# Two token tiles of the output product as seven half-size block products

## The chip, the cores and the metric

One Trainium2 chip, of which this kernel uses one core. A core has TensorE (PE: matmuls, with its weight loads shown apart as PEld), VectorE (DVE), ScalarE (ACT), GpSimd (POOL) and SyncE (SP, which issues most of the transfers). The metric is the device time of one execution in microseconds (us); lower is better. Three runs of the kernel before gave 304.9, 305.29 and 306.08 us, median 305.29.

## The reference

Attention in which a query sees only the keys whose nearest centroid is the same as its own, then a two-layer network with the SiLU gate. There are 4 batches, 8 heads, 768 tokens, a head size of 64 and 16 centroids a head; the network goes from 512 to 2048 to 512.

```python
q_assign = np.argmax(np.einsum('bhsd,hcd->bhsc', q_n, c_n), axis=-1)
k_assign = np.argmax(np.einsum('bhsd,hcd->bhsc', k_n, c_n), axis=-1)
mask = q_assign[:, :, :, None] == k_assign[:, :, None, :]
scores = np.where(mask, scale * np.matmul(q, k.transpose(0, 1, 3, 2)), -1000000000.0)
attn = softmax(scores)
x = np.matmul(attn, v).transpose(0, 2, 1, 3).reshape(B * S, H * D)
h = x @ w_in
g = h * (1.0 / (1.0 + np.exp(-h)))
return (g @ w_out).astype(np.float32)
```

Here q_n, k_n and c_n are the rows divided by their lengths, and softmax stands for the reference's lines with the maximum taken off. All inputs and the output are float32; the kernel works in f16 with f32 sums.

## The kernel before

**Stages.** The work goes by half batches (b, c): batch b of 4, half c of 2, 384 query tokens each, so eight half batches. For each of them:

- *Preparation of a head* (a Job): `load` brings raw rows of q and k as f32 (tile raw, eight buffers). `hi` and `lo` split them into two f16 parts (tile hl), `xpose` turns them by a transposing DMA, `logits_1` multiplies with the centroids, `lsum`, `mx_n` and `ge_n` find the cluster. Its one-hot code goes into the transposed rows (tile ab), by `c_scale`, `c_xpose` and `c_move` for batches 2 and 3, by `cd_mm` and `cd_ev` otherwise. So the mask is part of the score matmul.
- *Scores* (`qk_mm`, line 343): 192 units, 24 a half batch, each of two matmuls of 384 columns, and `exp` (line 348) on ScalarE for each. Two PSUM buffers of two banks are used in turn.
- *Values* (`pv`, line 360): 36 matmuls of 65 columns for two heads. The 65th column is a column of ones of the value tile vt and gives the sum of the softmax. `norm` divides (lines 370 and 372), and `xn_d` (a transposing DMA) or `xn_t` and `xn_ev` (TensorE and a copy) turn the result into xt.
- *Gate blocks* (`unit_a`, line 410): 16 blocks of 128 of the 2048 inner features, four matmuls of 384 columns each. `tanh` (line 430, ScalarE) and `gate` (line 433, VectorE) give (tanh(h/2) + 1) * h, which is twice the SiLU value, into gt (two buffers, 16 x 384 elements a partition).
- *Output* (`part_b`, line 468): for each of three tiles t of 128 tokens, 16 matmuls of 512 columns (gt block as weights, wout_s as the moving side) add up in one PSUM bank, in four pieces of four matmuls. Line 475 multiplies by 0.5 into ot, and SyncE sends it (line 477).

**Order.** Nothing is ordered by the engines themselves: each executes its instructions in the order in which the program issues them, and the program is written out flat. The opening is a list by hand (`plan`, line 657) up to unit 27 and the first eight gate blocks. Then a planner in the same file takes over (lines 690 to 947). It keeps a clock for each engine, and `choice` takes the engine that can start next. For TensorE, `options` lists the pieces that could go: scores when due (by PACE, LEAST, GAIN and the stock of other work), values, gate blocks and output pieces, each with a rank, the time at which its inputs are there and a length. `add` puts a piece on another engine's lane with the time when it is ready and how late it may be. `date` ties loads, preparation and casts to a unit's number. `sent` counts an output's time on SyncE. Four PSUM banks are shared by ph, pO, po, px and psN (`bank`, `done`); `po_on` says whether an output tile is open. What remains at the end is issued by lines 948 to 993: the gate blocks of the last half batch in pairs (`unit_aa`), its outputs, and the very last tile in three column pieces.

Half batches use gt in turn: gate blocks of one cannot begin while outputs of the one two before are left (line 882).

Of the kernel before, what the change touches and what calls it, by code (L numbers as in the profile page):

```python
# [34 lines left out]
def kernel(  # L35
# [64 lines left out]
    raws, hls, abs_ = {}, {}, {}  # L100

    def load(job, eng=nc.sync):
        raw = mp.tile([128, 12, D], f32, name="raw", tag="raw", bufs=8)
        for dst, ap in job.srcs:
            o = raw[:, dst, :]
            if len(ap.shape) == 2:
                eng.dma_start(o.rearrange("p n d -> p (n d)"), ap)  # L107
            else:
                eng.dma_start(o.rearrange("p (h n) d -> p h (n d)", h=4), ap)
        raws[job.name] = raw  # L110

    def hi(job, eng=None, part=None):
        s = part or slice(0, job.n)
        if job.name not in hls:
            hls[job.name] = mp.tile([128, 12, 2, D], f16, name="hl", bufs=4)
        o, i = hls[job.name][:, s, 0, :], raws[job.name][:, s, :]
        if eng == "act":
            nc.scalar.activation(out=o, in_=i, func=AF.Copy, bias=0.0, scale=QS)  # L118
        elif eng == "pool":
            nc.gpsimd.tensor_scalar(out=o, in0=i, scalar1=QS, scalar2=None, op0=ALU.mult)  # L120
        else:
            nc.vector.tensor_scalar(out=o, in0=i, scalar1=QS, scalar2=None, op0=ALU.mult)  # L122
# [103 lines left out]
    def c_xpose(job):  # L226
        cd = cds[job.name] = mp.tile([128, 2, 128], f16, name="cdt", bufs=4)
        nc.sync.dma_start_transpose(cd, ohd[nn[job.name] % 3].rearrange("p h n -> p (h n)"))  # L228
# [16 lines left out]
    def cd_ev(job, eng):  # L245
        m = (job.n + 1) // 2
        cd = mp.tile([6 * HC, 256], f16, name="cd", bufs=4)
# [173 lines left out]
    def unit_a_end(b, c, fb, ph):  # L421
# [7 lines left out]
        def tanh():  # L429
            nc.scalar.activation(out=tn, in_=ph[:, 0:HALF], func=AF.Tanh, bias=0.0, scale=0.5)  # L430
# [12 lines left out]
    def unit_aa(b, c, fb):  # L443
# [8 lines left out]
        def act():  # L452
            tn = mp.tile([128, 2, HALF], f32, name="tn2", tag="raw", bufs=8)
            nc.scalar.activation(out=tn, in_=ph[:, :, 0:HALF], func=AF.Tanh, bias=0.0, scale=0.5)
# [8 lines left out]
    def part_b(b, c, t, n, bk=3):  # L463
# [9 lines left out]
        def act():  # L473
            ot = mp.tile([128, DM], f32, name="ot", bufs=3)
            nc.vector.tensor_scalar(out=ot, in0=po, scalar1=0.5, scalar2=None, op0=ALU.mult)  # L475
# [3 lines left out]
        return act  # L479

# [30 lines left out]
    for vt in vtb:  # L511
        nc.vector.memset(vt[:, :, D : D + 1], 1.0)
# [182 lines left out]
    PACE, LEAST, GAIN = 1.40, 12, .03  # L695
    HOLD = 6

# [23 lines left out]

    dates = {}
# [6 lines left out]
    def chain(job, b):  # L729
        def split(t):  # L730
# [4 lines left out]
            add("DVE", t, 0.5, lambda: hi(job), lambda t: add("DVE", t, 0.9, lambda: lo(job), turned, 1.5), 1.5)  # L735
# [19 lines left out]
        def out_of_bank(t):  # L755
            add("DVE", t + 0.2, 0.44, lambda: cd_ev(job, "D"), lambda t: known(max(clock["SP"], t) + 1.0), 0.3)
# [31 lines left out]
    for i in range(H, B * H):  # L788
# [8 lines left out]
        date(p, lambda t, i=i: cast(i, t))  # L797
    for od in ohd:
        date(60, lambda t, od=od: add("POOL", t, 0.3, lambda: nc.gpsimd.memset(od, 0.0)))
# [8 lines left out]
    turn, po_on = 0, None  # L808
# [6 lines left out]
    def norm_piece(n, t):  # L815
# [10 lines left out]
        def after(t):  # L826
            if by_dma(n):
                add("SP", t, 1.28, lambda: xn_d(i, c), lambda t: ready(lands(t, 0.61) + 1.5))
            else:
                tensor_todo.append((t + 0.06, 0.17, lambda: xn_t(i, c), lambda t: add("DVE", t + 0.2, 0.3, lambda: xn_ev(i, c, "D"), ready)))  # L830

        add("DVE", t + 0.2, 0.72, lambda: norm(i, c), after)

    def unit_piece():
# [3 lines left out]
        def gated(t):  # L838
            gate_at[b, c, fb] = t

        def then(t):
# [10 lines left out]
    def part_piece():  # L852
        nonlocal po_on
        it = qb.pop(0)
        f = part_b(*it, None)
        po_on = it[:3] if it[3] < 3 else None

        def then(t):
            if f:
                add("DVE", t + 0.2, 0.62, f, sent)  # L860

        return then

    def options(t):
# [20 lines left out]
        if qb and (po_on or bank_at is not None):  # L885
            b, c, t_, n = qb[0]
            need = [gate_at.get((b, c, fb)) for fb in range(4 * n, 4 * n + 4)]
            a_soon = qa and x_at[qa[0][:2]] <= t + 0.5
            if None not in need and (len(qb) > HOLD or not a_soon):
                found.append((3 if turn < 4 else 2, max(need + ([] if po_on else [bank_at])), 0.863, "b"))  # L890
        return found

    def tensor_piece(o):
# [17 lines left out]
        elif what in ("a", "b"):  # L911
            turn = (turn + 1) % 7
            box = []
            run("PE", r, length, lambda: box.append(unit_piece() if what == "a" else part_piece()), lambda t: box[0](t))
# [33 lines left out]
    late = []  # L948
    while qa:
# [3 lines left out]
        if qb:  # L953
            f = part_b(*qb.pop(0), None)
# [3 lines left out]
    for fb in range(0, NFB, 4):  # L958
        for n, unit in ((0, unit_aa), (2, unit_a), (3, unit_a)):
# [3 lines left out]
            if qb and n != 2:  # L963
                f = part_b(*qb.pop(0), None)
# [4 lines left out]
    for x in qb:  # L969
        f = part_b(*x, None)  # L970
# [10 lines left out]
    for w in (5 * DM // 8, DM // 4, DM // 8):  # L981
# [10 lines left out]
        nc.vector.tensor_scalar(out=ot[:, cs_], in0=po[:, 0:w], scalar1=0.5, scalar2=None, op0=ALU.mult)  # L992
# [29 lines left out]
```

## Time and profile before

| | |
|---|---|
| median of 3 runs | 305.29 us |
| profiled execution, span from first to last instruction | 302.8 us |
| matmuls of line 468 (output tiles), 368 of 512 columns | 90.8 us busy |
| matmuls of line 343 (scores), 384 of 384 columns | 93.2 us busy |
| matmuls of line 410 (gate blocks), 480 of 384 columns | 92.4 us busy |
| matmuls of line 360 (values), 1152 of 65 columns | 41.2 us busy |
| tanh (line 430) and gate (line 433), 120 each | 60.1 and 64.0 us busy |
| DMA | 44.07 MB, mean 146 GB/s |

The profile is of one execution and counts its time from the first instruction to the last; the runs' times hold also what lies around it. Matmuls overlap in the records: a row's mean is longer than the distance from one start to the next, so prices of matmuls are best taken from stretches where one kind stands alone. A row of the groups reads: line, engine, operation, output and input tiles, shapes, count, then busy time in us and the mean in ns, then the idle time of the engine before these instructions and what ended it. In the chain and the timeline, a row gives the start, the length and how many instructions were merged. A row of the waits gives who waited for whom, the total, how often, and the longest.

### The profile page before, as it was taken

The page shows a single profiled execution, that of the slowest core. Times are in us where ns is not written, and L with a number is a line of the kernel's source. Part 1 is how long each engine was busy: PE and PEld are TensorE (multiplying, and loading weights), DVE is VectorE, ACT ScalarE, POOL GpSimd, SP SyncE. Part 2 cuts the span into 40 slices and gives each one's busy share as a digit, 9 for nine tenths or more (in the row PEclk, how much of TensorE's full clock was granted, in tenths as well). Part 3 has the DMA queues.
Part 4 walks back from the last instruction along what each step waited for, and adds up shares of the span by engine and source line. Part 5 has one row for each costly group of instructions (what it writes and reads, how often), then busy time and mean ns, then how long its engine had stood idle before and what let it go on. Part 6 is the DMA issues. An engine that isn't in the chain of part 4 may idle for free.

```text
span 302.8 us, 7783 instructions
## 1 busy us (share of the span) xinstructions
PE 294.3 (97%) x3113; PEld 186.3 (62%) x3113; DVE 200.6 (66%) x427; ACT 211.2 (70%) x341; POOL 69.1 (23%) x131
## 2 busy tenths in 40 slices
PE   7899989999999999999999999999999999999995
PEld 3777756566675566655666556655666556755644
DVE  5987669699995679855889468873464136522732
ACT  5899889653985688955698468955897568951520
POOL 2984700101310141433333324122100000000000
PEclk9999999999999999999999999999999999999999
DMA  7888999999794879869999998953101120010102
GB/s 212 249 185 183 201 254 209 247 252 223 174 184 117 218 188 151 197 160 176 231 187 226 187 179 211 163 82 97 38 0 55 46 82 13 16 50 35 37 35 69
DMA packets 74387, 44.07 MB, mean 146 GB/s; under 512 B 54352, under 2 KB 69360, under 8 KB 74352
## 3 DMA queue, kind: packets, MB, share of 16 engines
q1 hardware_dynamic: 69264, 35.16, 50.8%
q0 software_dynamic: 4800, 8.13, 14.2%
q8 instruction: 24, 0.39, 0.6%
q10 hardware_dynamic: 288, 0.30, 0.3%
q14 instruction: 11, 0.09, 0.1%
HBM read 27.30 MB, written 6.29 MB: 111 GB/s over the span
## 4 chain that ended last, share of the span: by engine, by line
PE 87%; ACT 4%; DVE 4%; DMA 2%; SPq 1%; issue 1%; DVEq 0%; ACTq 0%
PE ph L410 25%; PE po L468 25%; PE pS L343 19%; PE pO L360 11%; PE psN L175 3%; ACT P L348 3%; PE phs L448 2%; DVE hl L127 1%; PE po L986 1%; DMA raw<-in_k_dram 1%; DMA xt<-xn 1%; SPq L107 1%; ACT ab L159 1%; PE px L382 0%; SPq L228 0%
## 5 line engine op out<-in xcount | busy, mean ns | idle before, releaser
L348 ACT ACTIVATE P<-pS 128x768 f16<-128x768 f32 x192 | 155.6, 821 | 55.1 <-PE pS L343 54.7
L343 PE MATMUL pS<-ab 128*128 128x384 f16 x384 | 93.2, 326 | 0.5 <-ACT P L348 0.4
L410 PE MATMUL ph<-xt,win_s 128*128 128x384 f16 x480 | 92.4, 326 | 1.2 <-DVE gt L433 0.8
L468 PE MATMUL po<-wout_s,gt 128*128 128x512 f16 x368 | 90.8, 379 | 0.0
L433 DVE SCALAR_TENSOR_TENSOR gt<-tn,ph 128x384 f16<-128x384 f32 x120 | 64.0, 549 | 23.7 <-ACT tn L430 23.1
L430 ACT ACTIVATE tn<-ph 128x384 f32<-128x384 f32 x120 | 60.1, 507 | 10.1 <-PE ph L410 8.1
L410 PEld LDWEIGHTS <-win_s 128*128 128x128 f16 x480 | 46.2, 98 | 31.4 <-issue 2.0
L468 PEld LDWEIGHTS <-gt 128*128 128x128 f16 x368 | 35.0, 98 | 33.8
L343 PEld LDWEIGHTS <-ab 128*128 128x128 f16 x384 | 34.7, 98 | 26.1 <-issue 1.1
L360 PEld LDWEIGHTS <-P 128*128 128x128 f16 x1152 | 39.8, 97 | 4.4
L360 PE MATMUL pO<-vt,P 128*128 128x65 f16 x1152 | 41.2, 193 | 0.0
L127 DVE SCALAR_TENSOR_TENSOR hl<-raw,hl 128x768 f16<-128x768 f32 (+3 forms) x35 | 31.9, 916 | 0.8 <-ACT hl L118 0.4
L475 DVE TENSOR_SCALAR ot<-po 128x512 f32<-128x512 f32 x23 | 15.8, 688 | 23.3 <-PE po L468 23.1
L290 POOL CAST vt<-vn 128x384 f16<-128x384 f32 x32 | 17.9, 558 | 46.4 <-DMA vn<-in_v_dram 41.9
L187 DVE TENSOR_REDUCE L<-psN 128x192 f32<-128x384 f32 (+1 forms) x27 | 14.9, 550 | 15.1 <-PE psN L175 15.0
L232 POOL DMA_DIRECT2D ab<-cdt x16 | 8.9, 557 | 58.0 <-PE pS L343 28.0
L175 PEld LDWEIGHTS <-ab 128*128 128x128 f16 x458 | 17.2, 97 | 5.0 <-DMA ab<-hl 1.1
L175 PE MATMUL psN<-stk,ab 128*128 128x32 f16 (+1 forms) x458 | 18.6, 188 | 0.5 <-DMA ab<-hl 0.5
L370 DVE RECIPROCAL zr<-pO 128x6 f32<-128x6 f32 x32 | 6.2, 193 | 19.2 <-PE pO L360 18.8
L372 DVE TENSOR_TENSOR xn<-pO,zr 128x384 f16<-128x384 f32 x32 | 17.8, 557 | 1.1
L219 POOL TENSOR_SCALAR od<-od 128x96 f16<-128x96 f16 x16 | 9.2, 576 | 36.0 <-DVE od L212 35.9
L122 DVE TENSOR_SCALAR hl<-raw 128x768 f16<-128x768 f32 x24 | 13.9, 580 | 0.6 <-DMA raw<-in_k_dram 0.6
(75 smaller groups left out, 155.8 us busy)
## 6 DMA issues: line engine op xcount, KB each, us to landing
raw<-in_k_dram SPq DMA_DIRECT2D x31, 192.0 KB, 3.8
out_dram<-ot SPq DMA_DIRECT2D x23, 256.0 KB, 2.3
raw<-in_q_dram SPq DMA_DIRECT2D x24, 192.0 KB, 3.6
vn<-in_v_dram SPq DMA_DIRECT2D x16, 192.0 KB, 4.5
vn<-in_v_dram POOLq DMA_DIRECT2D x16, 192.0 KB, 3.7
win_s<-in_moe_w_in_dram POOLq DMA_DIRECT2D x8, 256.0 KB, 6.7
wout_s<-in_moe_w_out_dram POOLq DMA_DIRECT2D x4, 512.0 KB, 18.2
raw<-in_q_dram SPq DMA_DIRECT2D x2, 384.0 KB, 4.3
```

The costliest lines, as they stand in the source:

```text
L127: nc.vector.scalar_tensor_tensor(out=hl[:, s, 1, :], in0=raws[job.name][:, s, :], scalar=QS, in1=hl[:, s, 0, :], op0=ALU.mult, op1=ALU.sub ...
L175: nc.tensor.matmul(L[:, n % g, :, n // g], ab[:, i, :], stk[:, job.groups[i // 3][0], x : x + w], start=(x == 0), stop=(x + w == 2 * HC),)
L290: nc.gpsimd.tensor_copy(vt[:, :, 0:D], vns.pop(i))
L343: nc.tensor.matmul(pS[:, e, 0:HALF], abs_[kj.name][:, kn, :], rhs, start=True, stop=True)
L348: nc.scalar.activation(out=P, in_=pst.pop(u)[:, :, 0:HALF], func=AF.Exp, bias=0.0, scale=ESC)
L360: nc.tensor.matmul(o[:, (2 * t + h) * VW : (2 * t + h + 1) * VW], Ps[i + h, c, j // 2][:, j % 2, ts(t, 128)], vtb[(i + h) % 13][:, j, 0:VW ...
L372: nc.vector.tensor_tensor(out=xn, in0=ov[:, :, 0:D], in1=zr.unsqueeze(2).to_broadcast([128, 2 * NM, D]), op=ALU.mult)
L410: nc.tensor.matmul(ph[:, 0:HALF], win_s[:, r, ts(fb, 128)], xts[b, c][:, r, :], start=(r == 0), stop=(r == NR - 1))
L430: nc.scalar.activation(out=tn, in_=ph[:, 0:HALF], func=AF.Tanh, bias=0.0, scale=0.5)
L433: nc.vector.scalar_tensor_tensor(out=gt[:, fb, :], in0=tn, scalar=1.0, in1=ph[:, 0:HALF], op0=ALU.add, op1=ALU.mult)
L468: nc.tensor.matmul(po, gts[b, c][:, fc, ts(t, 128)], wout_s[:, fc, :], start=(fc == 0), stop=(fc == NFB - 1))
L475: nc.vector.tensor_scalar(out=ot, in0=po, scalar1=0.5, scalar2=None, op0=ALU.mult)
```

## The change

For five of the eight half batches, (1,0) to (3,0), the first two of the three token tiles are computed together. Their 256 tokens x 2048 features times 2048 x 512 are cut into 2 x 2 blocks, and Strassen's scheme in Winograd's form gives the product by seven block products instead of eight, each of 8 matmuls of 256 columns. For this

- VectorE forms four sums of gt blocks a pair (`sums`): S1 and S2 in a new tile sg, S3 and S4 in place in gt;
- VectorE forms four differences of wout blocks once, in ten pieces from unit 72 on (`tw_piece`); they lie in five raw slots that later loads no longer use (these have three), and two of 32 blocks in zz;
- products add up in two PSUM banks, X and Y. ScalarE copies product 1 to ot (`p1`) and, after products 6 and 5, the whole of X to a tile uu (`u2`); VectorE adds them to the outputs (`c11`, `c22`, `c12`). Product 6 waits for `p1`, product 7 for `u2`, product 4 for `c22`, product 3 for `c22` and S4;
- the two tiles leave in two transfers, one of 512 columns side by side and one of two pieces of 256 columns a row. The third tile goes as before, and its pieces may be taken ahead of a product that is not ready.

The factor of a half moves: the column of ones in vt becomes 2.0, so that x is halved, tanh takes scale 1.0, and the outputs are copied without a factor. The planner may now put some casts and copies on ScalarE or VectorE (`either`), by which has less before it; four of its constants are changed. Tiles hl and cd share fewer buffers after the first 18 jobs. The list of the opening stays.

```diff
+    EARLY = H + 2 + H
+    def raw_tag(n):
+        return f"raw{n % 8 if n < EARLY else 5 + n % 3}"
...
-        raw = mp.tile([128, 12, D], f32, name="raw", tag="raw", bufs=8)
+        raw = mp.tile([128, 12, D], f32, name="raw", tag=raw_tag(n), bufs=1)
...
-            nc.scalar.activation(out=tn, in_=ph[:, 0:HALF], func=AF.Tanh, bias=0.0, scale=0.5)
+            nc.scalar.activation(out=tn, in_=ph[:, 0:HALF], func=AF.Tanh, bias=0.0, scale=1.0)
...
+    TW = ((0, 0, 6), (0, 6, 2), (1, 0, 4), (1, 4, 4), (2, 0, 2), (2, 2, 4), (2, 6, 2), (3, 0, 2), (3, 2, 4), (3, 6, 2))
...
+    def tw_piece(n, f, m):
+        if n * HK + f < 30 and len(tws) <= (n * HK + f) // 6:
+            tws.append(mp.tile([128, 6, HD], f16, name="tw", tag=f"raw{len(tws)}", bufs=1))
+        ks, us = slice(f, f + m), slice(HK + f, HK + f + m)
+        lo_, up = slice(0, HD), slice(HD, DM)
+        a = wout_s[:, ks if n == 0 else us, lo_ if n == 3 else up]
+        b_ = tw(0, f, m) if n == 2 else tw(2, f, m) if n == 3 else wout_s[:, ks, up if n else lo_]
+        nc.vector.tensor_tensor(out=tw(n, f, m), in0=a, in1=b_, op=ALU.subtract)
...
+        def sums(self, k):
...
+            o, x, y, op = (
+                (s1, a21, a22, ALU.add), (s2, s1, a11, ALU.subtract), (a21, a11, a21, ALU.subtract), (a12, a12, s2, ALU.subtract)
+            )[k - 1]
+            nc.vector.tensor_tensor(out=o, in0=x, in1=y, op=op)
+
+        def product(self, k):
+            gt, lo_, up = self.gt, slice(0, HD), slice(HD, DM)
+            if k == 1:
+                self.X = bank("po")
+            if k == 2:
+                self.Y = bank("po2")
+            o = self.Y[:, lo_] if k == 2 else self.X[:, up if k in (5, 3) else lo_]
+            for f in range(HK):
...
+                nc.tensor.matmul(o, w, x, start=(f == 0 and k in (1, 2)), stop=(f == HK - 1), skip_group_check=True)
+
+        def p1(self):
+            self.ot = mp.tile([128, DM], f32, name="ot", bufs=3)
+            nc.scalar.activation(out=self.ot[:, HD:DM], in_=self.X[:, 0:HD], func=AF.Copy, bias=0.0, scale=1.0)
+
+        def c11(self):
+            nc.vector.tensor_tensor(out=self.ot[:, HD:DM], in0=self.Y[:, 0:HD], in1=self.ot[:, HD:DM], op=ALU.add)
+            done(self.Y)
+
+        def u2(self):
+            nc.scalar.activation(out=uus[0][:, HD : HD + DM], in_=self.X, func=AF.Copy, bias=0.0, scale=1.0)
...
+        def c22(self):
+            nc.vector.tensor_tensor(out=self.ot[:, 0:HD], in0=self.X[:, 0:HD], in1=uus[0][:, DM : DM + HD], op=ALU.add)
+            o, x = self.rows()
+            nc.sync.dma_start(o[:, x + HD : x + HD + DM], self.ot)
+
+        def c12(self):
+            ot = mp.tile([128, DM], f32, name="ot", bufs=3)
+            nc.vector.tensor_tensor(out=ot, in0=self.X, in1=uus[0][:, 0:DM], op=ALU.add)
+            done(self.X)
...
-        nc.vector.memset(vt[:, :, D : D + 1], 1.0)
+        nc.vector.memset(vt[:, :, D : D + 1], 2.0)
...
-    PACE, LEAST, GAIN = 1.40, 12, .03
+    PACE, LEAST, GAIN, WORK = 1.34, 12, .03, 20.05
     HOLD = 6
+    MARGIN = 0.3
+    EARLY_T = 72
...
+    def backlog(eng, t):
+        return max(clock[eng] - t, 0.0) + sum(p[2] for p in lanes[eng] if p[0] <= t + 1.0)
+
+    def either(ready, dve, act, f, then=None, late=0.0):
+        eng = "ACT" if backlog("ACT", ready) + act + MARGIN < backlog("DVE", ready) + dve else "DVE"
+        add(eng, ready, act if eng == "ACT" else dve, lambda: f(eng[0]), then, late)
...
+    paired = {(b, c) for b in range(B) for c in range(2)} - {(0, 0), (0, 1), (B - 1, 1)}
...
-                qb.extend((b, c, t_, n) for t_ in range(NM) for n in range(4))
+                if (b, c) in paired:
+                    pairs[b, c], at[b, c] = Pair(b, c), {}
+                    qb.extend([(b, c, "p", k) for k in (1, 2, 6, 5, 7, 4, 3)] + [(b, c, NM - 1, n) for n in range(4)])
+                else:
+                    qb.extend((b, c, t_, n) for t_ in range(NM) for n in range(4))
...
+            names = {6: ("c1", "s2"), 5: ("s1",), 7: ("u2", "s3"), 4: ("c22",), 3: ("c22", "s4")}[n]
+            need = [at[b, c].get(x) for x in names] + [tw_ready(n)]
...
-        if unit < NU and unit - 2 in exp_at and 6 * pv_next > unit - 15:
+        if unit < NU and unit - 2 in exp_at and 6 * pv_next > unit - 11:
...
-                stock = 1.302 * len(qa) + 0.863 * len(qb) + 20.8 * (unit // 24 - released)
-                due = t >= scored + min(max(PACE + GAIN * (stock - LEAST - 0.867 * (24 - unit % 24)), 0.8), 2.2)
+                stock = 1.253 * len(qa) + 0.868 * len(qb) + WORK * (unit // 24 - released)
+                due = t >= scored + min(max(PACE + GAIN * (stock - LEAST - WORK / 24 * (24 - unit % 24)), 0.8), 2.2)
...
+            ahead = next((k for k, q in enumerate(qb) if (q[2] == "p") != (qb[0][2] == "p")), None)
+            for k in (0, ahead):
+                if k is not None and (k or opened or len(qb) > HOLD or not a_soon):
+                    r = part_ready(qb[k], bank_at)
+                    if r is not None:
+                        found.append((3.5 if k else 3 if turn < 4 else 2, r, 0.874 if qb[k][2] == "p" else 0.863, ("b", k)))
```

More of the change, by code (lines that the diff above doesn't have):

```diff
@@ L839, in gated @@
             gate_at[b, c, fb] = t
+            if fb == NFB - 1 and (b, c) in paired:
+                if all("over" in at[x] for x in pairs if x != (b, c)):
+                    sums_from(b, c, t)
+                else:
+                    next_pair.append((b, c))
         def then(t):
@@ L948, with tail_part @@
     late = []
+    def tail_part():
+        it = qb.pop(0)
+        if it[2] != "p":
+            return part_b(*it, None)
+        pr, k = pairs[it[:2]], it[3]
+        if k in (2, 6, 7, 4):
+            while late:
+                late.pop(0)()
+        pr.product(k)
+        return {1: pr.p1, 2: lambda: (pr.c11(), pr.sums(4)), 5: pr.u2, 7: pr.c22, 3: pr.c12}.get(k)
     while qa:
```

149 lines of the change are left out of this document (121 added, 28 removed).

## The prediction

> **What bounds the kernel now.** I read the page's busy table, then the chain that ended last, then the busy time by stages, and last TensorE's waits. From the page:
>
> ```profile
> span 302.8 us, 7783 instructions
> PE 294.3 (97%) x3113; PEld 186.3 (62%) x3113; DVE 200.6 (66%) x427; ACT 211.2 (70%) x341; POOL 69.1 (23%) x131
> PE 87%; ACT 4%; DVE 4%; DMA 2%; SPq 1%; issue 1%; DVEq 0%; ACTq 0%
> ```
>
> TensorE is named first by both. A busy share can hide idle stretches, so here is the busy time in stages of about one half batch each (length, then PE, PEld, DVE, ACT and POOL busy, clock, DMA share, GB/s):
>
> ```profile
> 36.00:65.00 29.00, 28.16 (x280) 17.57 (x277) 21.96 (x43) 21.94 (x37) 2.16 (x5) 1.00 1.19 234
> 65.00:98.00 33.00, 32.74 (x349) 20.86 (x348) 28.61 (x61) 22.73 (x37) 4.92 (x11) 1.00 0.83 186
> 98.00:131.00 33.00, 33.00 (x392) 21.73 (x390) 26.91 (x55) 26.37 (x42) 9.97 (x19) 1.00 0.86 184
> 131.00:164.00 33.00, 32.34 (x343) 20.19 (x342) 23.74 (x47) 24.34 (x39) 13.25 (x25) 1.00 0.96 200
> 164.00:197.00 33.00, 33.00 (x331) 20.34 (x327) 23.97 (x48) 23.39 (x38) 9.68 (x22) 1.00 0.91 186
> 197.00:230.00 33.00, 33.00 (x327) 20.48 (x326) 17.49 (x36) 24.44 (x42) 4.91 (x11) 1.00 0.24 53
> 230.00:264.00 34.00, 34.00 (x311) 20.52 (x309) 14.52 (x28) 25.39 (x42) 0.00 (x0) 1.00 0.14 44
> ```
>
> From 36 to 264 us TensorE is idle for 0.84 + 0.26 + 0.66 = 1.76 us, and the granted clock is 1.00. So in these stages nothing but TensorE sets the pace, and a matmul taken away there is worth its whole length, as long as the planner keeps the engine fed. Its waits after the opening, and the chain's last pieces:
>
> ```profile
> PE ph L410 <- DVE gt L433: 0.8, 1, 0.8
> PE psN L175 <- DMA ab<-hl: 0.5, 1, 0.5
> 273.96 1.10 PE pO L360 x36
> 287.78 1.30 PE ph L410 x8
> 289.08 6.91 PE po L468 x32
> 295.99 3.55 PE po L986 x48
> ```
>
> Two waits in 267 us. The last 21 us are matmuls back to back, and the change leaves those of the last half batch as they are.
>
> **The change part by part.**
>
> *Matmuls.* The last chain rows give prices without gaps: 6.91 / 32 = 0.2159 us for 512 columns, 1.30 / 8 = 0.1625 for 384. The slope is 0.0534 / 128 = 0.417 ns a column, so 256 columns cost 0.2159 - 0.1068 = 0.1091 us. Is the weight load a floor, now that 56 loads stand where 32 did? The pO row has a load for every 65-column matmul and goes at 1.10 / 36 = 0.031 us each, so a load does not hold a matmul of 0.109. Two token tiles of one half batch cost 32 x 0.2159 = 6.91 us before and 56 x 0.1091 = 6.11 after: 0.80 us less. In five half batches that is 4.0 us. The third tile, the first two half batches and the last are as before.
>
> *Vector work that is added.* Each pair adds four sums of 1024 f16 elements, all operands in SBUF, and three additions from PSUM; once, there are ten weight pieces of together 8192 elements. It removes two copies of 512. No row shows an f16 sum. The nearest:
>
> ```profile
> L127 DVE SCALAR_TENSOR_TENSOR hl<-raw,hl 128x768 f16<-128x768 f32 x26 | 25.2, 970 | 0.3
> L127 DVE SCALAR_TENSOR_TENSOR hl<-raw,hl 128x384 f16<-128x384 f32 x1 | 0.6, 559 | 0.4 <-ACT hl L118 0.4
> L161 DVE COPY ab<-pTk 128x768 f16<-128x768 f16 x7 | 3.8, 549 | 0.5 <-PE pTk L150 0.5
> L393 DVE COPY xt<-px 128x384 f16<-128x384 f16 x10 | 3.4, 353 | 2.7 <-PE px L382 2.5
> L475 DVE TENSOR_SCALAR ot<-po 128x512 f32<-128x512 f32 x23 | 15.8, 688 | 23.3 <-PE po L468 23.1
> L372 DVE TENSOR_TENSOR xn<-pO,zr 128x384 f16<-128x384 f32 x32 | 17.8, 557 | 1.1
> ```
>
> Two inputs, one of them f32: (970 - 559) / 384 = 1.07 ns an element and 148 ns fixed, so 1.24 us for a sum. All 16-bit, one input: (549 - 353) / 384 = 0.51 ns and 157 ns fixed, so 0.68 us. I take 0.68, since the operands are all 16-bit as in that row, and keep 1.24 as the other end. Twenty sums are 13.6 us (24.8), the pieces 10 x 0.157 + 8192 x 0.00051 = 5.7 us (10.2). The additions follow the L372 row, 557 ns at 384 and 1.07 a further element: 0.42 us at 256, 0.69 at 512. A pair is then 4 x 0.68 + 2 x 0.42 + 0.69 - 2 x 0.69 = +2.9 us of VectorE (5.1 at the slow end).
>
> A rule bears on the choice: the Trainium skill, "VectorE: DVE Perf Modes", "The perf-mode tier table", has a 16-bit tensor_tensor in SBUF at two elements a cycle, 1224 ns for 2048. My estimate by that page is 0.7 us a sum; with f32 operands its rate is one a cycle, with which the 970 ns row agrees. By either end TensorE's sum stays the same; what hangs on it is the chance of the VectorE rival below.
>
> *Scalar work that is added.* Per pair a copy of 256 and one of 512 from PSUM:
>
> ```profile
> L348 ACT ACTIVATE P<-pS 128x768 f16<-128x768 f32 x192 | 155.6, 821 | 55.1 <-PE pS L343 54.7
> L430 ACT ACTIVATE tn<-ph 128x384 f32<-128x384 f32 x120 | 60.1, 507 | 10.1 <-PE ph L410 8.1
> L122 DVE TENSOR_SCALAR hl<-raw 128x768 f16<-128x768 f32 x24 | 13.9, 580 | 0.6 <-DMA raw<-in_k_dram 0.6
> ```
>
> The slope is 314 / 384 = 0.82 ns: 0.40 and 0.61 us, +1.0 us a pair.
>
> *Where that lies.* The last scores of all, in the order of time:
>
> ```profile
> 271.75 0.49 PE L343 MATMUL pS<-ab 128*128 128x384 f16 x2
> 272.07 1.89 PE L468 MATMUL po<-wout_s,gt 128*128 128x512 f16 x8
> ```
>
> The first 27 of the 192 units are written out by hand, up to about 36 us, so 165 units take 271.8 - 36 = 236 us, 1.43 each, and unit 72, at which the weight pieces may begin, comes near 100 us. They fall into the stage 98:131: 26.9 + 5.7 = 32.6 of 33 us of VectorE. This would be full, but the new choice of engine may send some five casts of 580 ns and an output copy of 688 to ScalarE, where I take them at 0.82 and 0.61: VectorE comes to 29.0, ScalarE from 26.4 to 31.1. The pairs (1,0) and (1,1) fall into 131:197, where VectorE has 9 us free a stage; the other three lie after 197, with 15 us or more free. So I cost all of this at nothing: the cover is TensorE's own stock of work. Without it the stage 98:131 would lengthen by what VectorE lacks, up to 26.9 + 10.2 - 5 x 0.58 - 33 = 1.2 us with slow sums.
>
> *Waits that are added.* Product 6 waits for ScalarE's copy of product 1 (product 2, 8 x 0.109 = 0.87 us, stands between and covers 0.2 + 0.40, the 0.2 being what the planner counts from a matmul to its reader). Product 7 waits for the 512 copy after product 5: 0.2 + 0.61 us. Product 4 waits for the 256 addition after product 7: 0.2 + 0.42 us. Behind a late product every matmul on TensorE waits in order, scores included, and for those ScalarE's exponentials. The cover is whatever the planner puts between: a gate block, scores, or a quarter of the third tile. After the last gate block there are only scores and output blocks, as in the two rows above. The third tile gives four pieces of 4 x 0.216 = 0.86 us and the two gaps need 0.81 + 0.62 us, so one piece in each gap is enough unless the copy stands behind an exponential of 821 ns. Bounds per pair: zero with full cover (nothing in these waits can gain), 1.43 us with none. I take 0.2, near the covered end, because four pieces stand against two gaps: 5 x 0.2 = 1.0 us.
>
> *Storage and queues.* The later loads have three raw slots for eight. A slot is held from the load's issue to the end of the difference that reads it:
>
> ```profile
> 132.67 0.85 SPq L107 DMA_DIRECT2D raw<-in_q_dram  x1
> 139.27 0.77 SPq L107 DMA_DIRECT2D raw<-in_q_dram  x1
> 140.10 1.30 DVE L127 SCALAR_TENSOR_TENSOR hl<-raw,hl 128x768 f16<-128x768 f32 x1
> ```
>
> That is 8.7 us, with a new load every 6.6, so two slots are in use and the third is spare; the same spacing serves three hl slots and four shared code slots. No gain, no cost; were a load to wait for its slot, SyncE would hold what is queued behind it, the transposes of the attention output above all. The halves taken out of the gate (scale 1.0, ones of 2.0, plain copies) change no instruction's size. SyncE sends three outputs a half batch as before, of the same bytes. The memset on GpSimd is one of 256 columns, in a stage where POOL is idle for 23 of 33 us.
>
> *Sum.* 302.8 - 4.0 + 1.0 = 299.8 us of span. The median of the runs, 305.29, lies 2.5 us above the profiled span; what lies around the span is untouched, so I forecast 302.3 us. For these runs, 0.5% (1.5 us) is about what a measurement can tell from no change.
>
> **The rivals.**
>
> *The handover gaps stay open (slower).* If the planner's order leaves nothing between products 5, 7 and 4, or a ScalarE copy lands behind an exponential, each pair pays up to 1.43 us, and 0.82 more for that exponential. At 1.43 us the time is 302.8 - 4.0 + 7.2 + 2.5 = 308.5, at 2.25 it is 312.6. It turns slower than before beyond 0.80 us a pair. For it: VectorE and ScalarE run strictly in the written order, with 23 to 26 of 33 us taken on ScalarE in each stage from 65 to 230. Against it: a wait for one of them is in the profile once (0.8 us).
>
> *The saving goes at the turn of half batches (no change).* The planner's filler between two half batches is shorter by 0.80 us, and if the chain score, exponential, values, transpose is what ends last there, TensorE simply waits longer:
>
> ```profile
> 143.53 0.52 PE L175 MATMUL psN<-stk,ab 128*128 128x32 f16 x12 [0.51 <-DMA ab<-hl]
> 140.08 1.67 SPq L107 DMA_DIRECT2D raw<-in_k_dram  x1
> 143.19 1.20 SPq L401 DMA_TRANSPOSE xt<-xn  x1
> ```
>
> Here it ran dry once, behind a load on SyncE. All five turns together give back 4.0 us: 302.8 + 1.0 + 2.5 = 306.3, at least 305.3. Against it: the planner is told of the shorter work (20.05 for 20.8) and asks for scores earlier (1.34 for 1.40).
>
> *VectorE becomes the bound from 98 to 197 us.* With 1.24 us a sum, the stage 98:131 lacks 1.2 us, and the two pairs behind it bring 10.2 us to 66 us with 18 free, which holds: 302.3 + 1.2 = 303.5. There may also be collisions:
>
> ```profile
> 126.68 0.98 DVE L127 SCALAR_TENSOR_TENSOR hl<-raw,hl 128x768 f16<-128x768 f32 x1
> 126.80 1.22 POOL L290 CAST vt<-vn 128x384 f16<-128x384 f32 x1
> 134.76 0.51 POOL L290 CAST vt<-vn 128x384 f16<-128x384 f32 x1
> ```
>
> A GpSimd cast of 0.51 us takes 1.22 beside a two-input VectorE instruction, and the new sums are of that kind. GpSimd is busy for 30% of the stage 98:131; if each of the ten weight pieces loses 0.71 us when it meets GpSimd, that is 10 x 0.30 x 0.71 = 2.1 us more: 305.6. Against it: it takes the slow end of the sums, and TensorE's stock covers what is only late. The Trainium skill, "SBUF — State Buffer", "Who interferes with whom", states it so: a VectorE instruction with two SBUF inputs and a GpSimd one that reads SBUF hold each other up; the trace agrees.
>
> *More than forecast.* The gaps are all covered and the new order loses the two old waits too: 302.8 - 4.0 - 1.3 + 2.5 = 300.0.
>
> **How the numbers follow.** Forecast 0.51 (its own range 301.0 to 303.7), more than forecast 0.11, turns 0.18, open handovers 0.15, VectorE 0.05. Faster by over 0.5% (under 303.76) are the first two: 0.62. Within are the turns and VectorE, less a little that ends slower: 0.21. Slower (over 306.82): 0.17. The range goes from 300.3 to 306.6: it leaves out the handovers and the very end of the gain.
>
> **What would show it.** The product rows should have 256 columns, 280 of them at 0.109 us start to start, and 160 rows of 512 fewer. A sum should take 0.68 us. TensorE's waits should name the X copy or the 256 addition, in total about 1 us; were they 4 or more, the handover rival is right. A wait for xt<-xn or an idle stretch ahead of ph at the turns would show the second rival; gate blocks waiting for gt between 98 and 131 us the third. The prediction is wrong if 256 columns cost over 0.12 us, or if TensorE's idle after 36 us grows by more than 2.5 us.

## The result, and the profile after

| | before | changed |
|---|---|---|
| median of the runs beside each other | 305.24 us (8 runs) | 301.64 us (8 runs, 301.25 to 304.23) |
| ratio | | 0.9897, 95% interval 0.987 to 0.9924 |
| repeated later | 305.23 us (23 runs) | 302.43 us (6 runs), ratio 0.9916, 0.9888 to 0.9945 |
| profiled execution: run, span | span 302.8 us | 302.92 us, span 300.7 us |

So the change makes the kernel faster by 2.8 to 3.6 us, about 1%; 302.3 was forecast. In three of the experiments below some executions ran in a slower state of the chip; their medians are of the others. The changed kernel's page, its first line, its busy times and its chain by engine:

```profile
span 300.7 us, 8083 instructions
PE 290.8 (97%) x3233; PEld 197.8 (66%) x3233; DVE 216.1 (72%) x455; ACT 219.6 (73%) x358; POOL 72.4 (24%) x132
PE 81%; DMA 7%; DVE 4%; ACT 4%; issue 1%; POOL 1%; SPq 1%; POOLq 0%; DVEq 0%
```

TensorE is still busy for 97%. The DMA share of 7% was 2% before, and it lies in the opening, which is the same list in both kernels. The chain's two longest pieces of it (start, length, what):

```profile
6.06 3.95 DMA raw<-in_q_dram
21.89 6.88 DMA ab<-cd
```

In this execution the first gate block of the hand-written list starts at 37.49 us, in the one before at 35.35. So the planned part has to be looked at by itself. Here is the time from that gate block to the last matmul, for the kernel before, the changed one, and a second execution of the changed one (length, then PE, PEld, DVE, ACT and POOL busy, clock, DMA share, GB/s):

```profile
35.35:299.52 264.17, 262.41 (x2595) 162.62 (x2592) 172.11 (x341) 181.51 (x292) 45.06 (x92) 1.00 0.64 138
```

```profile
37.49:297.66 260.17, 258.57 (x2715) 174.03 (x2712) 186.72 (x369) 189.62 (x309) 47.28 (x93) 1.00 0.65 140
```

```profile
36.18:296.61 260.43, 258.48 (x2715) 174.09 (x2712) 186.36 (x369) 189.51 (x309) 45.45 (x93) 1.00 0.65 139
```

This is the account to read. The length is TensorE's busy time and its idle time: 264.17 = 262.41 + 1.76 before, 260.17 = 258.57 + 1.60 and 260.43 = 258.48 + 1.95 after. The busy time fell by 3.84 and 3.93 us, the idle time moved by -0.16 and +0.19. VectorE carries 14 us more and ScalarE 8, and none of it shows. TensorE's waits after the opening, in the changed kernel:

```profile
PE ph L416 <- DVE gt L439: 0.8, 1, 0.8
PE po L546 <- DVE gt L439: 0.6, 1, 0.6
```

No product waits for ScalarE's copy (uu) or for the addition (ot). One waits for a gate block. In the second execution the waits are of the same kind, 0.8, 0.5 and 0.5 us. The stages from 98 to 264 us in the changed kernel show where the added work went:

```profile
98.00:131.00 33.00, 33.00 (x393) 21.80 (x391) 26.81 (x54) 27.81 (x45) 11.49 (x21) 1.00 0.88 193
131.00:164.00 33.00, 32.44 (x365) 22.78 (x364) 28.92 (x59) 25.59 (x42) 12.23 (x21) 1.00 1.02 207
164.00:197.00 33.00, 33.00 (x364) 23.11 (x360) 26.72 (x55) 25.76 (x42) 11.46 (x25) 1.00 0.84 180
197.00:230.00 33.00, 33.00 (x358) 23.17 (x356) 20.30 (x40) 25.57 (x43) 4.46 (x10) 1.00 0.25 60
```

VectorE stands at 26.7 to 28.9 of 33 us in the first three, where it stood at 23.7 to 26.9 before. The groups with the new operations:

```profile
L530 DVE TENSOR_TENSOR sg<-sg,gt 128x1024 f16<-128x1024 f16 x5 | 3.8, 762 | 0.1
L530 DVE TENSOR_TENSOR gt<-gt,sg 128x1024 f16<-128x1024 f16 x5 | 3.4, 684 | 0.0
L557 ACT ACTIVATE uu<-po 128x512 f32<-128x512 f32 x5 | 3.0, 597 | 2.0 <-PE po L546 1.9
L564 DVE TENSOR_TENSOR ot<-po,uu 128x256 f32<-128x256 f32 x5 | 2.1, 423 | 4.8 <-PE po L546 4.8
L550 ACT ACTIVATE ot<-po 128x256 f32<-128x256 f32 x5 | 1.9, 384 | 1.4 <-PE po L546 1.4
L128 DVE TENSOR_SCALAR hl<-raw 128x768 f16<-128x768 f32 x22 | 12.8, 580 | 1.2 <-DMA raw<-in_k_dram 1.2
```

A sum takes 0.68 us where nothing meets it (684; why one sg<-sg,gt takes longer is told at the end), the copies 0.60 and 0.38, the addition 0.42. And the one chain row of two products side by side gives the price of 256 columns (the chain in the order of time: start, length, what):

```profile
268.60 1.75 PE po L546 x16
```

1.75 / 16 = 0.109 us each.

### The profile page after: what moved, and what is told of

Read it like the earlier page. It is cut to its first block, busy times and chain, and to the rows that moved or that the text cites. A ratio compares the mean times of both kernels' runs of the same rounds, so it can differ in the third digit from the quotient of the medians.

```text
span 300.7 us, 8083 instructions
## 1 busy us (share of the span) xinstructions
PE 290.8 (97%) x3233; PEld 197.8 (66%) x3233; DVE 216.1 (72%) x455; ACT 219.6 (73%) x358; POOL 72.4 (24%) x132
## 4 chain that ended last, share of the span: by engine, by line
PE 81%; DMA 7%; DVE 4%; ACT 4%; issue 1%; POOL 1%; SPq 1%; POOLq 0%; DVEq 0%
PE ph L416 22%; PE pS L349 17%; PE po L474 15%; PE pO L366 10%; PE po L546 10%; DMA ab<-cd 3%; DMA raw<-in_q_dram 3%; ACT P L354 3%; PE psN L181 2%; PE phs L454 2%; DVE hl L133 1%; DVE gt L439 1%; DMA raw<-in_k_dram 1%; PE po L1188 1%; POOL hl L126 1%
## 5 line engine op out<-in xcount | busy, mean ns | idle before, releaser
L474 PE MATMUL po<-wout_s,gt 128*128 128x512 f16 x208 | 52.2, 379 | 0.0
L474 PEld LDWEIGHTS <-gt 128*128 128x128 f16 x208 | 19.7, 98 | 18.0
L296 POOL CAST vt<-vn 128x384 f16<-128x384 f32 x32 | 19.4, 606 | 47.1 <-DMA vn<-in_v_dram 47.1
L546 PEld LDWEIGHTS <-gt 128*128 128x128 f16 x200 | 19.3, 98 | 5.5 <-issue 0.8
L546 PE MATMUL po<-wout_s,gt 128*128 128x256 f16 x120 | 15.5, 272 | 0.6 <-DVE gt L439 0.6
```

The costliest lines, as they stand in the source:

```text
L296: nc.gpsimd.tensor_copy(vt[:, :, 0:D], vns.pop(i))
L474: nc.tensor.matmul(po, gts[b, c][:, fc, ts(t, 128)], wout_s[:, fc, :], start=(fc == 0), stop=(fc == NFB - 1))
L546: nc.tensor.matmul(o, w, x, start=(f == 0 and k in (1, 2)), stop=(f == HK - 1), skip_group_check=True)
```

## The experiments

Twelve runs. The first kind leaves the changed kernel's order of instructions as it is, since the planner is not told of the edit; the second kind changes what the planner sees, so that it writes another order. Medians are compared with 301.6 and 302.4 us, the two medians of the changed kernel; ratios are to the kernel before.

### The changed kernel again

> The changed kernel once more, beside the three runs below. Theory: ratio 0.987 to 0.992 as on record; from the first planned gate blocks to the last matmul 4.0 to 4.5 us less than before, and the rest of the spread from run to run lies in the opening, which is the same list in both kernels.

Measured: 302.43 us, ratio 0.9916 (0.9888 to 0.9945). The planned part is 3.7 us shorter than before (260.43 for 264.17), a little under the 4.0 to 4.5 expected, and 4.0 in the first execution. The two executions' spans differ by 1.1 us (300.7 and 299.6), and that lies in the opening (37.49 and 36.18), as expected. It does not explain the two medians, of which the second is the higher one.

### Product 2 twice (same order)

```diff
-            for f in range(HK):
+            for f in list(range(HK)) * (2 if k == 2 else 1):
```

> Product 2 is computed twice in each pair, the second time from a cleared bank: 5 x 8 more matmuls of 256 columns, of which the planner knows nothing. Theory (after 36 us TensorE's time counts in full): +5 x 0.873 = 4.4 us on 301.6, 306.0 us, ratio 1.002. Rival (TensorE has slack in the pairs, waits at the handovers would hide part of it): +2 us or less, ratio up to 0.995.

Measured: 306.19 us, ratio 1.0031 (1.0002 to 1.0059), so 3.8 to 4.6 us more for 4.37 us of matmuls. The planned part:

```profile
36.31:300.06 263.75, 262.81 (x2755) 177.94 (x2752) 186.75 (x369) 189.58 (x309) 48.38 (x93) 1.00 0.63 138
```

Busy 262.81 - 258.5 = 4.3 us more; idle 0.94, against 1.6 to 1.95 in the changed kernel. So in this execution the part is 3.3 to 3.6 us longer: about four fifths of TensorE's added time count, by the medians nearly all of it. The rival (slack in the pairs, 2 us or less) falls.

### Product 4 left out (same order)

```diff
-            for f in range(HK):
+            for f in range(0 if k == 4 else HK):
```

> Product 4 is left out in each pair (8 matmuls of 256 columns; one quarter of the two tiles' output lacks its term), the planner counts its time as if it were there. Theory (TensorE is the only bound): 5 x 0.873 = 4.4 us less, 297.3 us. Rival (the freed time shows that ScalarE, VectorE or the turn of half batches is next): 1 to 3 us less, with new idle stretches of TensorE.

Measured: 298.44 us, ratio 0.9782 (0.9763 to 0.9801), 3.2 to 4.0 us less. The planned part:

```profile
35.60:293.00 257.40, 254.81 (x2674) 170.18 (x2672) 188.08 (x369) 189.26 (x309) 47.27 (x93) 1.00 0.63 141
```

Busy 3.7 us less, idle 2.59 us, up to 1.0 more. Other waits begin to show, of 0.2 to 0.8 us, mostly for a VectorE gate; they take up to a quarter of the gain, and this part is 2.8 to 3.0 us shorter. Between the theory (4.4) and the rival (1 to 3), nearer to the theory.

### The sums three times, the differences twice (same order)

```diff
-        nc.vector.tensor_tensor(out=tw(n, f, m), in0=a, in1=b_, op=ALU.subtract)
+        for _ in range(2):
+            nc.vector.tensor_tensor(out=tw(n, f, m), in0=a, in1=b_, op=ALU.subtract)
...
-            nc.vector.tensor_tensor(out=o, in0=x, in1=y, op=op)
+            for _ in range(3 if k < 3 else 1):
+                nc.vector.tensor_tensor(out=o, in0=x, in1=y, op=op)
```

> S1 and S2 are each computed three times in place of once and every weight difference twice, with the same results and without the planner's knowledge: 4 x 0.69 = 2.8 us more of VectorE a pair and 5.8 us once, 20 us in all, more than if all sums went at the slow end of 1.24 us. Theory (VectorE's additions lie beside TensorE's work): within 1 us of 301.6. Rival (VectorE is nearly the bound from 98 to 197 us): +3 us or more, with TensorE waiting for gt or for sg.

Measured: 322.37 us, ratio 1.0557 (1.0529 to 1.0586). Not within 1 us: the kernel is longer by as much as the work that was added. TensorE's longest waits:

```profile
PE po L548 <- DVE sg L532: 8.0, 3, 3.2
PE pO L366 <- DVE L L193: 2.8, 1, 2.8
PE psN L181 <- DVE ot L555: 1.7, 1, 1.7
PE ph L416 <- DVE gt L439: 1.5, 3, 0.8
```

Product 6 waits up to 3.2 us for S2, and other work waits for VectorE instructions queued behind the sums. TensorE's idle time from the first gate block on is 16.7 us, against 1.6 to 1.95. That is not the whole of the 20 us. After the two longest waits, 3.16 us (ended at 141.28) and 2.76 us (ended at 216.00), the granted clock was 0.70 to 0.73 in stretches of 3 us, and matmuls of 256 columns went at half their pace:

```profile
217.41 3.58 PE L548 MATMUL po<-tw,sg 128*128 128x256 f16 x16
```

The next matmul starts at 220.81: 3.40 / 16 = 0.213 us each, in place of 0.109. By the starts of the matmuls this took some 3.4 us in the two places. So the agreement of 20 us with 20 us is chance. The place was also badly chosen for a test of VectorE's time: S1 and S2 are a chain that product 6 waits for. The next run was made to take the two apart.

### As much VectorE work in other places (same order)

```diff
-        P = mp.tile([128, 2, HALF], f16, name="P", bufs=16)
+        P = mp.tile([128, 2, HALF], f16, name="P", bufs=15)
...
-        nc.vector.tensor_tensor(out=tw(n, f, m), in0=a, in1=b_, op=ALU.subtract)
+        for _ in range(2):
+            nc.vector.tensor_tensor(out=tw(n, f, m), in0=a, in1=b_, op=ALU.subtract)
...
             nc.vector.tensor_tensor(out=o, in0=x, in1=y, op=op)
+            for _ in range(5 if k == 4 else 0):
+                aside = mp.tile([128, 6, 128], f16, name="aside", tag="aside", bufs=1)
+                nc.vector.tensor_tensor(out=aside, in0=s1[:, 0:6], in1=s2[:, 0:6], op=ALU.add)
```

> As much more VectorE work as in the run with the sums three times, but where nothing waits for it first: five sums of 768 elements into a tile that nobody reads, after S4 of each pair (some 0.55 us each, 2.7 a pair), and every weight difference twice (5.8 us), 19 us in all; one score buffer fewer makes room. Theory (the 20 us lost there came from S2 being late for product 6, and VectorE has room otherwise): at most 5 us more than the changed kernel, with no wait of product 6 for sg. Rival (VectorE's time itself is the bound): 10 us more or over.

Measured: 312.61 us, ratio 1.0247 (1.0218 to 1.0275): 10 to 11 us more for 19 us of work. This is the rival's number, if only just: four of the five runs show a granted clock of 0.994 or 0.995, and the profiled one, at 1.00, took 310.19 us, 7.8 to 8.6 more. No product waits for sg. The two fullest stages, TensorE's waits, and VectorE's rows ahead of the first S3:

```profile
98.00:131.00 33.00, 30.21 (x343) 19.23 (x340) 29.86 (x59) 25.59 (x42) 11.16 (x18) 1.00 0.83 180
131.00:164.00 33.00, 30.03 (x344) 20.93 (x341) 30.39 (x61) 22.30 (x35) 14.86 (x25) 1.00 0.89 180
```

```profile
PE po L550 <- DVE zz L509: 2.3, 1, 2.3
PE po L550 <- DVE gt L531: 1.9, 2, 1.4
PE px L388 <- DVE xn L378: 0.9, 1, 0.9
PE ph L416 <- DVE xt L399: 0.9, 1, 0.9
138.63 3.38 DVE L534 TENSOR_TENSOR aside<-sg 128x768 f16<-128x768 f16 x5
142.34 0.68 DVE L531 TENSOR_TENSOR gt<-gt 128x1024 f16<-128x1024 f16 x1
```

TensorE is idle for 2.8 and 3.0 us in these two stages, and the waits account for it: from 98 to 131 us the division and a copy of the attention output stand behind weight differences that are formed twice (0.94 and 0.88 us), and three gates make up the rest; from 131 to 164 us product 4 waits 2.26 us for the last weight difference, and product 7 for S3, which stands behind the five added sums. So here too something waited for VectorE's queue, and the run does not measure VectorE's time alone.

Nor do the busy times give a share of VectorE at which the waits begin. From 65 to 98 us in the run with six half batches VectorE is at 30.55 of 33 us and TensorE idle for 0.35. The longer of product 7's two waits in the run here, 1.4 us at 278 us, lies in a stretch where VectorE is at 21.1 of 36 us. What decides is which result stands behind the added work. That VectorE's time by itself is a bound is not shown by this run.

### ScalarE's copy of X three times (same order)

```diff
-            nc.scalar.activation(out=uus[0][:, HD : HD + DM], in_=self.X, func=AF.Copy, bias=0.0, scale=1.0)
+            for _ in range(3):
+                nc.scalar.activation(out=uus[0][:, HD : HD + DM], in_=self.X, func=AF.Copy, bias=0.0, scale=1.0)
```

> ScalarE copies X to uu three times in place of once between products 5 and 7, 1.0 to 1.2 us longer at that handover in each of five pairs. Theory (the planner has put other work there that lasts longer than the copy): at most 2 us more than the changed kernel. Rival (the handovers are just covered): 5 us more.

Measured: 305.05 us (10 runs), ratio 1.0 (0.9971 to 1.003), 2.6 to 3.4 us more for some 5.5 us, with runs from 302.98 to 307.44. Between the two expectations. In the profiled execution, the fastest of them:

```profile
PE po L546 <- ACT uu L558: 1.2, 2, 0.8
PE po L546 <- DVE xn L378: 0.8, 1, 0.8
```

Two of the five handovers open, by 1.2 us together. So the cover at that handover is there, and it is not much longer than one more copy or two. What the slower executions waited for was not profiled.

### The third tile not taken ahead (new order)

```diff
-            for k in (0, ahead):
+            for k in (0,):
```

> The pieces of the third tile may no longer be taken ahead of a product that is not ready; they come after all seven. Theory (the covered handovers cost nothing because pieces of the third tile stand in them): where nothing else stands there, the two gaps of 0.81 and 0.62 us open, up to 1.43 us a pair, +2 to +7 us, 304 to 309 us. Rival (scores, values and gate blocks cover them anyway): within 0.5 us of 301.6.

Measured: 306.28 us, ratio 1.0032 (1.001 to 1.0053). The size is the theory's, the mechanism is not: products wait for the addition 0.2 us in all. The planned part, and TensorE's and VectorE's rows at the longest idle stretch:

```profile
35.96:301.04 265.08, 260.33 (x2714) 174.10 (x2712) 186.76 (x369) 189.76 (x309) 45.92 (x93) 1.00 0.61 137
```

```profile
159.46 0.81 PE L416 MATMUL ph<-xt,win_s 128*128 128x384 f16 x4 [2.19 <-DVE gt L439]
157.38 0.56 DVE L128 TENSOR_SCALAR hl<-raw 128x768 f16<-128x768 f32 x1 [2.28 <-DMA raw<-in_k_dram]
157.98 0.96 DVE L133 SCALAR_TENSOR_TENSOR hl<-raw,hl 128x768 f16<-128x768 f32 x1
158.86 1.01 DVE L439 SCALAR_TENSOR_TENSOR gt<-tn,ph 128x384 f16<-128x384 f32 x2
```

Read from below: two gates stand on VectorE behind a cast of raw rows that have not landed; without the gates the PSUM banks are not free, and TensorE stands for 2.19 us. The idle time is 4.75 us, some 3 more than in the changed kernel. The busy time is 1.8 us more for the same matmuls, and that is waiting too: a matmul of 384 columns stands in the records for 0.33 us, though the next one can start after 0.16, so every wait hides some 0.16 us in the busy time. By the starts of the matmuls, 18 steps here are over 0.08 us longer than the matmul's price, and 6 in the changed kernel.

### Without pairs, with the new pace (new order)

```diff
-    date(EARLY_T - 1, lambda t: add("POOL", t, 0.3, uu_tile))
...
-    date(EARLY_T, lambda t: tw_step(0, t))
...
-    paired = {(b, c) for b in range(B) for c in range(2)} - {(0, 0), (0, 1), (B - 1, 1)}
+    paired = set()
```

> No half batch is paired and no weight differences are formed; the planner's new constants, its choice of engine and the moved factors of a half stay. Theory (the gain is the 2048 columns a pair that TensorE no longer streams): the 4.0 us come back, near 305.5 us, ratio to before 0.998 to 1.006. Rival (the planner's constants and the choice of engine bring the gain): stays near 302, ratio 0.988 to 0.993.

Measured: ratio 1.0058 (1.0019 to 1.0097), with 9 runs from 305.02 to 309.04. The gain is gone, as the theory has it, and some more. The planned part:

```profile
35.60:300.38 264.78, 262.21 (x2594) 162.43 (x2592) 169.91 (x333) 185.96 (x300) 47.08 (x92) 1.00 0.64 137
```

TensorE's busy time is back at that of the kernel before (262.21 and 262.41). The profiled execution is one of the shorter ones, so what the longer ones lose is not shown.

### Without pairs, with the old pace (new order)

The edit of the run above, and in addition:

```diff
-    PACE, LEAST, GAIN, WORK = 1.34, 12, .03, 20.05
+    PACE, LEAST, GAIN, WORK = 1.40, 12, .03, 20.8
...
-        if unit < NU and unit - 2 in exp_at and 6 * pv_next > unit - 11:
+        if unit < NU and unit - 2 in exp_at and 6 * pv_next > unit - 15:
...
-                stock = 1.253 * len(qa) + 0.868 * len(qb) + WORK * (unit // 24 - released)
+                stock = 1.302 * len(qa) + 0.863 * len(qb) + WORK * (unit // 24 - released)
```

> As the run without pairs, and with the pace, the stock weights and the limit on scores ahead of the kernel before; what is left of the change is the choice of engine, the smaller buffers and the moved halves. Theory: ratio 0.997 to 1.003 (the choice of engine and the buffers are worth nothing while TensorE is full). Rival (the choice of engine helps by itself): ratio under 0.995.

Measured: 305.97 us, ratio 1.0023 (0.9993 to 1.0054). The planned part:

```profile
35.87:300.95 265.08, 262.12 (x2594) 162.50 (x2592) 168.91 (x334) 184.99 (x299) 46.02 (x92) 1.00 0.65 137
```

The choice of engine, the smaller buffers and the moved halves are worth nothing measurable by themselves. Together with the run above, the planner's part of the change is not what makes it faster.

### Only the last three half batches paired (new order)

```diff
-    paired = {(b, c) for b in range(B) for c in range(2)} - {(0, 0), (0, 1), (B - 1, 1)}
+    paired = {(2, 0), (2, 1), (3, 0)}
```

> Only the last three half batches of the five are paired. Theory: 0.80 us lost for each of the two others, 303.2 us, ratio 0.994. Rival (the two pairs in the stages where VectorE is fullest cost more than they bring): as fast as the whole change or faster, 301.6 us or less, ratio up to 0.988.

Measured: 306.28 us, ratio 1.0021 (0.9988 to 1.0054). Neither came out: three pairs should be worth 2.4 us, and nothing of it arrives. The planned part:

```profile
35.37:299.04 263.67, 260.34 (x2667) 169.49 (x2664) 183.27 (x359) 187.59 (x305) 44.43 (x93) 1.00 0.63 138
153.85 1.46 PE L416 MATMUL ph<-xt,win_s 128*128 128x384 f16 x8 [1.40 <-DVE gt L439]
151.78 0.56 DVE L128 TENSOR_SCALAR hl<-raw 128x768 f16<-128x768 f32 x1 [1.38 <-DMA raw<-in_k_dram]
```

The busy time did fall, by 2.1 us (262.41 - 260.34), and the idle time rose from 1.76 to 3.33, with 1.40 us in one place: a cast that waits for its rows, as in the run with the third tile, with gates behind it. The idle time takes 1.6 of the 2.1 us; the runs' median is another 1 us above this execution (305.3 us), which stays open.

### Six half batches paired (new order)

```diff
-    EARLY_T = 72
+    EARLY_T = 58
...
-    paired = {(b, c) for b in range(B) for c in range(2)} - {(0, 0), (0, 1), (B - 1, 1)}
+    paired = {(b, c) for b in range(B) for c in range(2)} - {(0, 0), (B - 1, 1)}
```

> The half batch (0,1) is paired too, and the weight differences begin at unit 58 for 72. Theory: 0.80 us less again, 300.8 us, ratio 0.985 to 0.987. Rival (VectorE, with 28.6 of 33 us taken from 65 to 98 us, cannot form the 5.8 us of differences in time there): 301.6 us or more, with TensorE waiting for gt or tw.

Measured: 305.99 us, ratio 1.0035 (1.001 to 1.0059): 3.6 to 4.4 us slower than five pairs. Its waits:

```profile
PE po L546 <- DVE tw L508: 1.7, 2, 1.4
PE pS L349 <- DMA ab<-cdt: 1.6, 1, 1.6
PE po L546 <- DVE gt L439: 1.3, 1, 1.3
PE pS L349 <- ACT P L354: 1.3, 3, 0.6
```

The rival's first wait is there, products that wait for the weight differences, and its 1.7 us alone are more than a sixth pair's 0.80. The others, for scores and a gate block, come with a new order; the idle time of the planned part is 7.7 us in all. This execution, 308.02 us, is one of the longer ones.

### PACE 1.36 (new order)

```diff
-    PACE, LEAST, GAIN, WORK = 1.34, 12, .03, 20.05
+    PACE, LEAST, GAIN, WORK = 1.36, 12, .03, 20.05
```

> Only the planner's PACE, 1.36 for 1.34: the same instructions in another order. Theory (the columns are worth 4.0 us in any order, and the order adds an idle time of TensorE that is drawn anew each time): 300.5 to 304 us, and the difference to 301.6 is TensorE's idle time after 36 us. Rival (the constant itself sets the time): within 0.5 us of 301.6.

Measured: 302.63 us (10 runs), ratio 0.9919 (0.9892 to 0.9946). The planned part:

```profile
36.15:297.25 261.10, 258.52 (x2715) 174.51 (x2712) 186.72 (x369) 189.93 (x309) 45.92 (x93) 1.00 0.63 140
```

The same busy time as the changed kernel (258.52), an idle time of 2.58 for 1.6 to 1.95. By the medians the order is worth 0.2 to 1.0 us here, too little to tell theory and rival apart, and the columns' gain is there in this order too.

## Why the prediction was right, point by point

- **TensorE sets the time after 36 us.** Shown at a fixed order: 4.37 us of matmuls added cost 3.8 to 4.6 us, taken away they gave 3.2 to 4.0.
- **The columns, -4.0 us.** Measured: TensorE's busy time falls by 3.84 and 3.93 us, and without pairs it is back (262.1 and 262.2). The price of 0.109 us for 256 columns is the row's, and the loads, now 98 ns before every 109, hold nothing up.
- **The handovers, +1.0 us.** This term was mis-sized: in the profile it is nothing. No product waits for uu or for the 256 addition, and the idle time is as before. The mechanism of the cover is real, since 1.1 us more at one handover opens it in two pairs of five in the execution profiled, and it is broader than I had it: in the order without the third tile ahead, other work stands in the gaps.
- **The sums, 0.68 us each.** Right: 684 ns. The rows with 16-bit operands were the right end. They fit what the Trainium skill says in "VectorE: DVE Perf Modes", "The perf-mode tier table", two elements a cycle, from which the prediction's estimate was 0.7 us.
- **Where VectorE's work lies.** Partly wrong. The weight differences did not all fall into 98:131; four of the ten come after 131 us, the last just ahead of product 4 of the first pair (start, length, engine, line):

```profile
108.48 1.01 DVE L508 TENSOR_TENSOR tw<-wout_s 128x1536 f16<-128x1536 f16 x1
142.93 0.68 DVE L508 TENSOR_TENSOR tw<-wout_s,tw 128x1024 f16<-128x1024 f16 x1
145.59 0.41 DVE L508 TENSOR_TENSOR zz<-wout_s,tw 128x512 f16<-128x512 f16 x1
```

  And `either` moved two casts to ScalarE in the whole kernel (24 became 22 on VectorE), none of them from 98 to 131 us, where five were counted on. VectorE did not overflow there (26.8 of 33 us) because the pieces came later; in the code they may be up to 9 us late, but no run tests whether that is what spread them.
- **"I cost all of this at nothing."** True of the change: 14 us more of VectorE and 8 of ScalarE leave TensorE's idle time as it was. But the prediction read the free part of 33 us as room, and priced its VectorE rival at 1.2 us, or 3.3 with collisions, for sums at the slow end, which are 20 x 0.56 + 4.5 = 16 us of work. About 20 us more, put in two ways, cost 8 to 11 and 20 us. That reading leaves out what stands behind the added work in VectorE's order, also where two fifths of a stage are free.
- **The sum.** 302.8 - 4.0 and no handover term gives 298.8 us of span, 301.3 with 2.5. The medians are 301.6 and 302.4, so 0.3 to 1.1 us are left. A part of that is a step of the prediction that failed: "what lies around the span is untouched". A run's time less its span is 1.8 to 1.9 us in all 23 later runs of the kernel before and 2.2 to 2.3 us in all 14 of the changed one, 0.4 us more. Why stays open; with PACE 1.36, the same instructions in another order, it is 1.7 to 1.8. The 2.5 us were these 1.8 and some 0.7 by which the profiled execution was shorter than the median run. From the median span of the 23 runs, 303.4 - 4.0 + 2.2 = 301.6, the first median; the second is 0.8 above it, which stays open. In the two executions shown the opening is later than before by 2.1 and 0.8 us (37.49 and 36.18 for 35.35); the same gate block starts between 35.37 and 36.31 in the other eleven profiles, so the 0.8 is within its spread and 37.49 is beyond it. That the forecast of 302.3 lies between the two medians is in part luck: a handover term of 1.0 that is nothing stands where these smaller ones belong.
- **The rivals.** The saving did not go at the turns (idle unchanged), and the open handovers did not come. The wait at the turn (ph for xt<-xn) does exist, 1.9 us, in the order without pairs at the old pace.

## What to carry to other kernels

When one engine is busy for 99% of a stage, price a change by that engine's work alone, and then ask of each other engine what stands behind the added work in its order: a result that is due there comes late, here even where two fifths of the stage were free. A test of an engine's room needs added work with nothing due behind it; the two placements here, 10 and 20 us for nearly the same amount, both had something behind them. Where a planner writes the order, an edit that it sees draws a new order whose idle time can be as large as the gain (three pairs for five kept nothing measurable), so take the terms apart by edits that leave the order as it is.

## What the runs showed of the hardware that was not expected

How much VectorE is held up by GpSimd, and when. The prediction's rows showed the GpSimd cast lengthened, beside a VectorE instruction that had started first. The longest sum, an S2, and the cast beside it:

```profile
202.30 1.06 DVE L530 TENSOR_TENSOR sg<-sg,gt 128x1024 f16<-128x1024 f16 x1
202.28 0.52 POOL L296 CAST vt<-vn 128x384 f16<-128x384 f32 x1
```

The cast starts 0.02 us earlier and takes its usual time, and the sum takes 0.37 us more than its 0.69. Two other runs show the same: with PACE 1.36 an S1 that started 0.05 us after a cast took 0.99 us, and in the changed kernel's second execution a weight difference that started 0.17 us after one took 0.89 for 0.69. Each lost some 0.13 us less than the time in which the two overlap. That fits what the Trainium skill says in "SBUF — State Buffer", "Who interferes with whom": the one that starts first goes through and the other waits. From 201.57 to 206.4 us TensorE waited for none of these sums, so it cost no time here.

The other is the granted clock after a wait, in the run with the sums three times: 0.70 to 0.73 in stretches of 3 us behind waits of 3.16 and 2.76 us, with matmuls at half their pace, and 1.00 behind the waits of 2.44 and 2.43 us in the same run (ended at 252.43 and 287.26). No other profile here has a wait as long as 2.7 us after the opening.
